# First block of a fused state-space and feed-forward kernel: running rows added by VectorE, branch stages respread

## The chip, the cores and the metric

The kernel runs on one core of a Trainium2 chip. The time is the device time of one execution in microseconds; the median of 3 runs of the kernel before is 490.83 us (490.7 to 491.28). Engines are named as in the profile: PE is TensorE (its weight loads are PEld), DVE is VectorE, ACT is ScalarE, POOL is GpSimd, SP is the queue that issues most DMAs.

## The reference

A sequence of L = 2048 tokens with D = 448 channels passes two branches, each behind a layer norm that is scaled and shifted by a modulation made from a vector `c`:

```python
mod = (_silu(c) @ w_mod).reshape(c.shape[0], 6, 1, -1)
sa, ca, ga, sb, cb, gb = (mod[:, 0], ..., mod[:, 5])
h = _layernorm(x, axis=-1) * (1 + ca) + sa
x = x + ga * _A_ref(h, ...)          # state-space convolution, N = 256 states, + h * Dskip
h = _layernorm(x, axis=-1) * (1 + cb) + sb
x = x + gb * _B_ref(h, w_gate, w_up, w_down)   # (silu(h @ w_gate) * (h @ w_up)) @ w_down, F = 1792
```

`_A_ref` forms `K[d, l] = Re sum_n C exp(l dt A) dt B` and convolves `h` with it causally, by FFT. Everything is float32.

## The kernel before, in words

**Tiles.** The 2048 tokens are 16 tiles of 128 rows (numbered 0 to 15) in six blocks of 2, 2, 3, 3, 3, 3 tiles. A block's tiles go through the feed-forward branch together (`ffn`), and while they do, the tiles of the *next* block go through the first branch in pieces put between. This case is about the first block: its feed-forward has tiles 0 and 1, and beside it run the first-branch stages of tiles 2 and 3, the "branch tiles".

**Feed-forward.** A loop over f = 0 to 13 (a "step") takes 128 of the 1792 hidden channels: `gate_up(f)` multiplies the transposed, normalised tokens by the gate and up weights on PE (L686; 22 matmuls into two PSUM banks of a ring of four, `bank`), ACT applies Silu (L701), DVE multiplies (L714), ACT casts the product to its high part (L717), DVE takes the low part (L718). Then `down(f-1)` (L730) adds the previous step's product with the down weights into the banks `dn`, in six matmuls per step with two tiles. High and low parts stand in for full float32 products. In the first block the weights are still being split: ACT casts gate and up weights (L120), DVE takes their remainders (L122, L124); the same for the down weights (L112, L114). So in the first block each step brings DVE five instructions of its own.

**First branch.** A flag computed on the chip selects the small path, which is the one that runs here: the kernel is taken as linear over the lag, so the convolution is two running sums over tokens. The stages of a branch tile i in the first block are: statistics of the first norm and their root on POOL (`n1.stat`, `n1.root`); `s0`, the normalised and modulated rows h (L184, L186); `s1`, the gated operands v0 = h * gm0 and v1 = h * gm1 (L859, on DVE); `s4f`, the sums over the tokens up to each row, as products with the triangle `tri` on PE, o in the bank `cv` from v0 (L897) and s in a ring bank from v1 (L896); `s5`, which carries the totals on and adds both sums to the tile. The totals of all earlier tokens are two "running rows" run0 and run1, row 0 of the tile `run`; they are added to every row as products of tri's first row with them (L898, L899: one row of operand, 448 columns). The carry copies the last rows of s (L908, ACT), adds o (L909, DVE) and moves row 127 of `run` to row 0 by a DMA that ACT's queue issues (L910). Then come the statistics of the second norm (`n2.stat`, L148 and L149), their root on POOL (`n2.root`, L165 to L172), the normalised tile on ACT (`make_xn`, L199), and after step 13's gate and up the transposes on PE (L206) with their evictions (L207 to L212), which the next block's first gate products need.

**What sets the order.** Each engine works its queue in the order in which the code is written; a wait at the head holds all that stands behind. The place of each stage is written out in numbers: `TIMES[b]` holds for block b the half-steps of the first statistics, of their root, of each stage of each branch tile (the last number is `n2.stat`), of the second root and of `make_xn`. A half-step h is step h // 2, behind `gate_up` and ahead of `down` where it is even, behind `down` where it is odd.

Of the kernel before, what the change touches and what calls it, by code (L numbers as in the profile page):

```python
# [12 lines left out]
OP = mybir.AluOpType  # L13
# [16 lines left out]


TIMES = (
# [3 lines left out]
)  # L36
# [16 lines left out]
def f32(ap):  # L53
    return ap.bitcast(F32)
# [3 lines left out]
def tile_kernel(ctx, tc, x, a_re, a_im, b_re, b_im, c_re, c_im, log_dt, dskip,  # L58
                wd, wgate_up, states, groups, vecs, dft, idft, out):
    nc = tc.nc  # L60
    sy, ve, sc, po, pe = nc.sync, nc.vector, nc.scalar, nc.gpsimd, nc.tensor
# [10 lines left out]
    def bank():  # L72
        t = psg.tile([128, 512], F32, name="bank")
        return t

    xs = {}
# [50 lines left out]
    tri = const.tile([128, 128], F32R)  # L127
    tok = const.tile([128, 1], F32)

    run = const.tile([128, 2, D], F32)  # L130
    run0, run1 = run[:, 0, :], run[:, 1, :]
# [49 lines left out]
    def make_h(h, i, part=None, ca=ca1, sh=sa):  # L181
        m, rs = n1.of[i][0:2]
        if part != 1:
            ve.scalar_tensor_tensor(h, xs[i], m, ca, op0=OP.subtract, op1=OP.mult)  # L184
        if part != 0:
            ve.scalar_tensor_tensor(h, h, rs, sh, op0=OP.mult, op1=OP.add)  # L186
# [57 lines left out]
    with tc.tile_pool(name="pre", bufs=1) as pre:  # L244
# [6 lines left out]
        for kind, q in ((n[0], n[1:]) for n in ORDER.split()):  # L251
# [3 lines left out]
            elif kind == "m":  # L255
                g, b = int(q[0]), (slice(0, 2 * D), slice(2 * D, NM))[int(q[1])]
# [52 lines left out]
        for q in range(2):  # L309
# [14 lines left out]
        h01, v0, v1, hd, h2 = ([pre.tile([128, w], t, name=f"{n}_{q}") for q in range(2)] for n, t, w in  # L324
                               (("h", F32, D), ("v0", F32, D), ("v1", F32R, D), ("hd", F32, D), ("h2", F32, 512)))
# [517 lines left out]
    def small_path(pools):  # L843
        work = pools.work
        vs = {}

        def s0(i):
            h = h_of(i)
            make_h(h, i)
            vs[i] = h  # L850

        def s1(i, on_v=False):
            h = vs[i]
            v0 = v0_of(i)
            v1 = work.tile([128, D], F32R, name="v1", bufs=2)
            for v, g in ((v0, gm0), (v1, gm1)):
                (ve if on_v else po).tensor_tensor(v, h, g, op=OP.mult)  # L859
            vs[i] = h, v0, v1  # L860

        def rows(i, on_v=False):
            h, v0, v1 = vs[i]
            ve.tensor_tensor(v0[0:1], v0[0:1], run0[0:1], op=OP.add)  # L864
            (ve if on_v else po).tensor_tensor(v1[0:1], f32(v1[0:1]), run1[0:1], op=OP.add)  # L865

        def s2(i, on_v=False):
            rows(i, on_v)
            h, v0, v1 = vs[i]
            vh = work.tile([128, D], F32R, name="vh")  # L870
            vl = work.tile([128, D], F32R, name="vl")
            sc.copy(vh, v0)  # L872
            ve.tensor_tensor(vl, v0, f32(vh), op=OP.subtract)
            vs[i] = h, vh, vl, v1

        def s3(i, on_v=False):
            h = vs[i][0]
            (ve if on_v else po).tensor_tensor(h, h, gd, op=OP.mult)

        def s4(i):  # L880
            h, vh, vl, v1 = vs[i]
            o = CV[:, 0:D]
            s = bank()[:, 0:D]
            pe.matmul(o, tri, vh, start=True, stop=False)  # L884
            pe.matmul(s, tri, v1, start=True, stop=True)  # L885
            pe.matmul(o, tri, vl, start=False, stop=True)  # L886
            ve.tensor_tensor(xs[i], h, xs[i], op=OP.add)
            vs[i] = o, s

        def s4f(i):
            h, v0, v1 = vs[i]
            o = CV[:, 0:D]
            s = bank()[:, 0:D]
            pe.matmul(s, tri, v1, start=True, stop=False)  # L896
            pe.matmul(o, f32(tri), v0, start=True, stop=False)  # L897
            pe.matmul(s, f32(tri[0:1, :]), run1[0:1], start=False, stop=True)  # L898
            pe.matmul(o, f32(tri[0:1, :]), run0[0:1], start=False, stop=True)  # L899
            s3(i, True)  # L900
            ve.tensor_tensor(xs[i], h, xs[i], op=OP.add)
            vs[i] = o, s

        def s5(i):
            o, s = vs.pop(i)
            if i + 1 < NT:
                e = slice(96, 128)
                sc.copy(run1[e], s[e])  # L908
                ve.scalar_tensor_tensor(run0[e], run1[e], 128.0, o[e], op0=OP.mult, op1=OP.add)  # L909
                sc.dma_start(run[0:1], run[127:128])  # L910
            ve.tensor_tensor(xs[i], xs[i], o, op=OP.add)
            ve.scalar_tensor_tensor(xs[i], s, tok, xs[i], op0=OP.mult, op1=OP.add)

        v = lambda g: lambda i: g(i, True)
        return lambda b: ((s0, v(s1), s4f, s5), (s0, v(s1), v(s2), v(s3), s4, s5),
                          (s0, s1, s2, s3, s4, s5))[min(b, 2)]

    def general_path(pools, y):
# [34 lines left out]
    with tc.If(rv > 0) as cond:  # L953
        with ExitStack() as es:
            pools = Pools(es)
            run_blocks(pools, small_path(pools))
# [65 lines left out]
```

## Time and profile before

| | us |
|---|---|
| median of 3 runs | 490.83 |
| the profiled execution | 490.99 |
| its span (first to last instruction on record) | 489.2 |
| PE busy | 481.9 (99% of the span) |
| DVE busy | 269.1 (55%) |
| ACT busy | 162.4 (33%) |
| POOL busy | 71.6 (15%) |
| the first block's loop on PE, from step 1 to the second block's first product | 41.74 to 98.88 |

The granted clock of PE is 0.997 over the span. In the rows of the timeline stand start, duration, engine, line, operation, output and inputs, shape and count; brackets hold the idle time of the engine before the row and what ended it.

### The profile page before, as it was taken

The page shows a single profiled execution, that of the slowest core. Times are in us where ns is not written, and L with a number is a line of the kernel's source. Part 1 is how long each engine was busy: PE and PEld are TensorE (multiplying, and loading weights), DVE is VectorE, ACT ScalarE, POOL GpSimd, SP SyncE. Part 2 cuts the span into 40 slices and gives each one's busy share as a digit, 9 for nine tenths or more (in the row PEclk, how much of TensorE's full clock was granted, in tenths as well). Part 3 has the DMA queues.
Part 4 walks back from the last instruction along what each step waited for, and adds up shares of the span by engine and source line. Part 5 has one row for each costly group of instructions (what it writes and reads, how often), then busy time and mean ns, then how long its engine had stood idle before and what let it go on. Part 6 is the DMA issues. An engine that isn't in the chain of part 4 may idle for free.

```text
span 489.2 us, 6961 instructions
## 1 busy us (share of the span) xinstructions
PE 481.9 (99%) x2765; PEld 452.4 (92%) x2765; DVE 269.1 (55%) x521; ACT 162.4 (33%) x350; POOL 71.6 (15%) x93
## 2 busy tenths in 40 slices
PE   8999999999999999999999999999999999999995
PEld 5649988999999999999999999999999999999995
DVE  4868999568885444634735553474555445222224
ACT  5665545622226112224411222531122161211111
POOL 2141001000000023411005150100623010000000
PEclk9999999999999999999999999999999999999998
DMA  8945662020000200000210000030000002000001
GB/s 311 405 166 151 226 198 87 21 95 1 0 3 3 93 1 0 2 1 2 73 41 1 2 0 2 0 114 1 0 2 1 1 0 76 21 1 0 1 0 62
DMA packets 12268, 26.50 MB, mean 54 GB/s; under 512 B 1858, under 2 KB 8131, under 8 KB 12227
## 3 DMA queue, kind: packets, MB, share of 16 engines
q1 hardware_dynamic: 11520, 25.79, 15.4%
q8 instruction: 23, 0.38, 0.3%
q10 hardware_dynamic: 706, 0.18, 0.2%
q14 instruction: 19, 0.15, 0.1%
HBM read 22.26 MB, written 3.67 MB: 53 GB/s over the span
## 4 chain that ended last, share of the span: by engine, by line
PE 95%; DMA 2%; DVE 1%; ACT 0%; SPq 0%; issue 0%; DVEq 0%
PE bank L686 59%; PE dn L730 27%; PE bank L225 2%; DMA wm<-in_w_mod_groups_dram 2%; PE bank L206 1%; PE dn L420 1%; DMA vec<-in_c_log_dt_dram 1%; PE bank L229 1%; PE cv L886 0%; PE cv L884 0%; PE bank L885 0%; PE cv L225 0%; PE bank L376 0%; PE bank L898 0%; DVE x L769 0%; PE cv L206 0%
## 5 line engine op out<-in xcount | busy, mean ns | idle before, releaser
L686 PE MATMUL bank<-hhi,gu 128*128 128x384 f32 (+1 forms) x1169 | 210.1, 318 | 0.0
L686 PEld LDWEIGHTS bank<-hhi,gu 128*128 128x128 f32 x1169 | 190.3, 188 | 3.2 <-issue 0.7
L686 PE MATMUL bank<-hlo,gu 128*128 128x384 f32 (+1 forms) x668 | 131.5, 318 | 0.0
L714 DVE TENSOR_TENSOR bank<-raw,bank 128x384 f32<-128x384 f32 (+1 forms) x69 | 36.9, 535 | 142.8 <-PE bank L686 127.6
L686 PEld LDWEIGHTS bank<-hlo,gu 128*128 128x128 f32 x668 | 109.6, 188 | 0.2 <-DVE hlo L212 0.2
L717 ACT CAST phi<-bank 128x384 fp32r<-128x384 f32 (+1 forms) x83 | 36.9, 445 | 144.7 <-DVE bank L714 144.7
L701 ACT ACTIVATE raw<-bank 128x384 f32<-128x384 f32 (+1 forms) x70 | 32.9, 469 | 121.1 <-PE bank L686 112.6
L718 DVE TENSOR_TENSOR plo<-bank,phi 128x384 fp32r<-128x384 f32 (+1 forms) x83 | 42.5, 512 | 37.5 <-ACT phi L717 37.5
L730 PE MATMUL dn<-wdh,phi 128*128 128x448 f32 x218 | 58.2, 368 | 0.0
L730 PE MATMUL dn<-wdh,plo 128*128 128x448 f32 x218 | 57.9, 366 | 0.0
L730 PE MATMUL dn<-wdl,phi 128*128 128x448 f32 x218 | 57.7, 366 | 0.0
L730 PEld LDWEIGHTS dn<-wdl,phi 128*128 128x128 f32 x218 | 40.9, 188 | 3.6
L730 PEld LDWEIGHTS dn<-wdh,plo 128*128 128x128 f32 x218 | 41.0, 188 | 3.5
L730 PEld LDWEIGHTS dn<-wdh,phi 128*128 128x128 f32 x218 | 38.4, 188 | 1.7 <-ACT run L908 0.7
L859 POOL TENSOR_TENSOR m<-m,gm 128x448 f32<-128x448 f32 x9 | 11.2, 1240 | 64.8 <-DVE m L186 55.3
L165 POOL TENSOR_SCALAR rsb<-mvb 128x3 f32<-128x3 f32 (+2 forms) x7 | 1.9, 275 | 120.5 <-DVE mvb L149 120.5
L165 POOL TENSOR_SCALAR rsa<-mva 128x3 f32<-128x3 f32 (+1 forms) x6 | 1.4, 231 | 105.5 <-DVE mva L149 105.5
L120 ACT CAST gu<-raw 128x1024 fp32r<-128x1024 f32 x14 | 14.6, 1045 | 0.0
L872 ACT CAST vh<-m 128x448 fp32r<-128x448 f32 x12 | 6.8, 568 | 22.3 <-DVE m L864 22.3
L865 POOL TENSOR_TENSOR v<-v,run 1x448 fp32r<-1x448 f32 x9 | 11.4, 1272 | 17.8 <-DMA run<-run 17.5
L225 PE MATMUL bank<-wm,cs 128*128 128x448 f32 x30 | 12.6, 550 | 0.2 <-DMA wm<-in_w_mod_groups_dram 0.2
L122 DVE TENSOR_TENSOR gu<-raw,gu 128x768 fp32r<-128x768 f32 x13 | 12.3, 950 | 0.0
(217 smaller groups left out, 433.5 us busy)
## 6 DMA issues: line engine op xcount, KB each, us to landing
raw<-in_B_w_gate_up_dram SPq DMA_DIRECT2D x14, 512.0 KB, 3.7
rawd<-in_B_w_down_dram SPq DMA_DIRECT2D x16, 224.0 KB, 3.8
x<-in_A_u_dram SPq DMA_DIRECT2D x12, 224.0 KB, 3.1
out_dram<-x SPq DMA_DIRECT2D x11, 224.0 KB, 1.9
wm<-in_w_mod_groups_dram SPq DMA_DIRECT2D x5, 448.0 KB, 8.1
wm<-in_w_mod_groups_dram SPq DMA_DIRECT2D x5, 336.0 KB, 7.9
rawd<-in_A_u_dram SPq DMA_DIRECT2D x4, 224.0 KB, 3.0
out_dram<-rawd SPq DMA_DIRECT2D x4, 224.0 KB, 1.9
```

What stands on the lines that cost most here:

```text
L120: sc.copy(wgu[j][:, :, 0:4, :], w)
L122: en.tensor_tensor(lo, w[:, :, 0:3, :], f32(hi), op=OP.subtract)
L225: pe.matmul(ps[:, 0:D], cs[:, k:k + 1].to_broadcast([128, 128]), w[:, k * D:(k + 1) * D], start=k == 0, stop=False)
L686: pe.matmul(ps[s][:, 0:n], w[:, s, a], (hlo if lo else hhi)[:, k, 0:n], start=first and q == 0, stop=end and q == len(ka) - 1)
L701: sc.activation(p[:, 0:n], ps[0][:, 0:n], AF.Silu)
L714: ve.tensor_tensor(ps[1][:, 0:n], p[:, 0:n], ps[1][:, 0:n], op=OP.mult)
L717: sc.copy(hi[:, 0:n], ps[1][:, 0:n])
L718: ve.tensor_tensor(lo[:, 0:n], ps[1][:, 0:n], f32(hi[:, 0:n]), op=OP.subtract)
L730: pe.matmul(dn[q][:, 0:D], u[:, cs], v, start=f == 0 and z == 0, stop=f == (NF - 3 if last else NF - 1) and z == 2)
L859: (ve if on_v else po).tensor_tensor(v, h, g, op=OP.mult)
L865: (ve if on_v else po).tensor_tensor(v1[0:1], f32(v1[0:1]), run1[0:1], op=OP.add)
L872: sc.copy(vh, v0)
```

## The change

The two one-row products of `s4f` (L898, L899) go. In their place the running rows are added on DVE to row 0 of v0 and v1 ahead of the products, by `rows`, which the later blocks already use (L864, L865). The last stage of a tile is cut in two: `s5f` holds the carry (`carry`, L903 to L905) and the addition of s times the token number (L910); `s6f` adds o (L914), multiplies h by `gd` (L878, until now in `s4f`) and adds it (L916). So the stages are six and not four, and `TIMES[0]` is a new table: the first root at half-step 2 and no longer 5; tile 2's stages at 4, 7, 9, 11, 11, 12 with its statistics at 13 (before: 5, 10, 15, 15 and 15); tile 3's at 8, 11, 16, 19, 19, 21 with its statistics at 22 (before: 9, 9, 18, 19 and 19); the second root at 22 (19); the normalised tiles at 24 and 25 (24 and 23).

```diff
 TIMES = (
-    ((1, 1), 5, ((5, 10, 15, 15, 15), (9, 9, 18, 19, 19)), 19, (24, 23)),
+    ((1, 1), 2, ((4, 7, 9, 11, 11, 12, 13), (8, 11, 16, 19, 19, 21, 22)), 22, (24, 25)),
...
         def s4f(i):
             h, v0, v1 = vs[i]
             o = CV[:, 0:D]
             s = bank()[:, 0:D]
-            pe.matmul(s, tri, v1, start=True, stop=False)
-            pe.matmul(o, f32(tri), v0, start=True, stop=False)
-            pe.matmul(s, f32(tri[0:1, :]), run1[0:1], start=False, stop=True)
-            pe.matmul(o, f32(tri[0:1, :]), run0[0:1], start=False, stop=True)
-            s3(i, True)
-            ve.tensor_tensor(xs[i], h, xs[i], op=OP.add)
-            vs[i] = o, s
-
-        def s5(i):
-            o, s = vs.pop(i)
+            pe.matmul(s, tri, v1, start=True, stop=True)
+            pe.matmul(o, f32(tri), v0, start=True, stop=True)
+            vs[i] = o, s, h
+
+        def carry(i, o, s):
             if i + 1 < NT:
                 e = slice(96, 128)
                 sc.copy(run1[e], s[e])
                 ve.scalar_tensor_tensor(run0[e], run1[e], 128.0, o[e], op0=OP.mult, op1=OP.add)
                 sc.dma_start(run[0:1], run[127:128])
+
+        def s5f(i):
+            o, s, h = vs[i]
+            carry(i, o, s)
+            ve.scalar_tensor_tensor(xs[i], s, tok, xs[i], op0=OP.mult, op1=OP.add)
+
+        def s6f(i):
+            o, s, h = vs.pop(i)
+            ve.tensor_tensor(xs[i], xs[i], o, op=OP.add)
+            s3(i, h, True)
+            ve.tensor_tensor(xs[i], h, xs[i], op=OP.add)
+
+        def s5(i):
+            o, s = vs.pop(i)
+            carry(i, o, s)
             ve.tensor_tensor(xs[i], xs[i], o, op=OP.add)
             ve.scalar_tensor_tensor(xs[i], s, tok, xs[i], op0=OP.mult, op1=OP.add)
...
-        return lambda b: ((s0, v(s1), s4f, s5), (s0, v(s1), v(s2), v(s3), s4, s5),
+        return lambda b: ((s0, v(s1), v(rows), s4f, s5f, s6f), (s0, v(s1), v(s2), v(s3), s4, s5),
                           (s0, s1, s2, s3, s4, s5))[min(b, 2)]
```

How the rows of the queues move is shown at three places. First PE at tile 2's sums; `v_...` and `m_78` are v1 and v0, `run` the running rows, `dn` and `gu` the down products and the gate and up weights. Before, behind `down` of step 7:

```order
L730 MATMUL dn_69<-wdh_659,plo 128x448
L896 MATMUL bank<-v_761,tri 128x448
L897 MATMUL cv<-m_78,tri 128x448
L898 MATMUL bank<-run,tri 128x448
L899 MATMUL cv<-run,tri 128x448
L686 MATMUL bank<-hhi,gu_657 128x256 x7
```

And in the changed kernel, behind `down` of step 5:

```order
L730 MATMUL dn_69<-wdh_559,plo 128x448
L896 MATMUL bank<-v_668,tri 128x448
L897 MATMUL cv<-m_78,tri 128x448
L686 MATMUL bank<-hhi,gu_557 128x256 x7
L686 MATMUL bank<-hlo,gu_557 128x256 x4
```

Two of the four products are gone, and the other two stand two steps earlier.

Second, DVE from step 4's end to step 5's end, where tile 3's `s0`, tile 2's row additions and the steps' own L114 to L124 meet (`x_74`, `x_75` are tiles 2 and 3; `wd` and `gu` the split weights). Before:

```order
L184 SCALAR_TENSOR_TENSOR m_78<-x_75,mva,ca_89 128x448
L186 SCALAR_TENSOR_TENSOR m_78<-m_78,rsa,sa 128x448
L859 TENSOR_TENSOR m_78<-m_78,gm_92 128x448
L859 TENSOR_TENSOR v_717<-m_78,g_91 128x448
L114 TENSOR_TENSOR wdl_607<-rawd_84,wdh_606 128x448
L714 TENSOR_TENSOR bank<-p,bank 128x256
L122 TENSOR_TENSOR gu_604<-raw_80,gu_604 128x2x384
L718 TENSOR_TENSOR plo<-bank,phi 128x256
L124 TENSOR_TENSOR gu_604<-raw_80,gu_604 64x2x128
L859 TENSOR_TENSOR m_78<-m_78,gm_92 128x448
L859 TENSOR_TENSOR v_761<-m_78,g_91 128x448
```

And now:

```order
L186 SCALAR_TENSOR_TENSOR m_78<-m_78,rsa,sa 128x448
L864 TENSOR_TENSOR m_78<-m_78,run 1x448
L865 TENSOR_TENSOR v_668<-v_668,run 1x448
L114 TENSOR_TENSOR wdl_611<-rawd_84,wdh_610 128x448
L714 TENSOR_TENSOR bank<-p,bank 128x256
L122 TENSOR_TENSOR gu_608<-raw_80,gu_608 128x2x384
L718 TENSOR_TENSOR plo<-bank,phi 128x256
L124 TENSOR_TENSOR gu_608<-raw_80,gu_608 64x2x128
L904 SCALAR_TENSOR_TENSOR run<-run,cv 32x448
L910 SCALAR_TENSOR_TENSOR x_74<-bank,tok,x_74 128x448
L859 TENSOR_TENSOR m_78<-m_78,gm_92 128x448
L859 TENSOR_TENSOR v_776<-m_78,g_91 128x448
```

The row additions stand where an `s1` stood, and carry and first addition of tile 2 have come into step 5, ahead of tile 3's `s1`.

Third, ACT in steps 11 to 13, where the normalised tiles (`raw_81`) are made between the steps' casts. Before:

```order
L717 CAST phi<-bank 128x256
L199 ACTIVATE raw_81<-x_75,ngb,rsb 128x448
L199 ACTIVATE raw_81<-x_75,ngb,rsb 128x64
L112 CAST wdh_963<-rawd_82 128x448
L701 ACTIVATE p<-bank 128x256
L717 CAST phi<-bank 128x256
L199 ACTIVATE raw_81<-x_74,ngb,rsb 128x448
L199 ACTIVATE raw_81<-x_74,ngb,rsb 128x64
L112 CAST wdh_1029<-rawd_83 128x448
```

And now:

```order
L112 CAST wdh_965<-rawd_82 128x448
L701 ACTIVATE p<-bank 128x256
L717 CAST phi<-bank 128x256
L199 ACTIVATE raw_81<-x_74,ngb,rsb 128x448
L199 ACTIVATE raw_81<-x_74,ngb,rsb 128x64
L199 ACTIVATE raw_81<-x_75,ngb,rsb 128x448
L199 ACTIVATE raw_81<-x_75,ngb,rsb 128x64
L112 CAST wdh_1017<-rawd_83 128x448
L701 ACTIVATE p<-bank 128x256
```

Both tiles are now made behind step 12's cast L717, ahead of step 13's L112 and Silu.

More of the change, by code (lines that the diff above doesn't have):

```diff
@@ L874, in s2, with s3 @@
             vs[i] = h, vh, vl, v1
-        def s3(i, on_v=False):
-            h = vs[i][0]
+        def s3(i, h=None, on_v=False):
+            h = vs[i][0] if h is None else h
             (ve if on_v else po).tensor_tensor(h, h, gd, op=OP.mult)
@@ L910, in s5 @@
                 sc.dma_start(run[0:1], run[127:128])
+        def s5f(i):
[10 more added lines that the diff above has]
+            carry(i, o, s)
             ve.tensor_tensor(xs[i], xs[i], o, op=OP.add)
             ve.scalar_tensor_tensor(xs[i], s, tok, xs[i], op0=OP.mult, op1=OP.add)
-        v = lambda g: lambda i: g(i, True)
-        return lambda b: ((s0, v(s1), s4f, s5), (s0, v(s1), v(s2), v(s3), s4, s5),
+        v = lambda g: lambda i: g(i, on_v=True)
+        return lambda b: ((s0, v(s1), v(rows), s4f, s5f, s6f), (s0, v(s1), v(s2), v(s3), s4, s5),
                           (s0, s1, s2, s3, s4, s5))[min(b, 2)]
```

## The prediction

> **What bounds the kernel now.** I read the page first, then the chain of waits, then the timeline of the first block engine by engine.
>
> ```profile
> PE 481.9 (99%) x2765; PEld 452.4 (92%) x2765; DVE 269.1 (55%) x521; ACT 162.4 (33%) x350; POOL 71.6 (15%) x93
> ...
> PE 95%; DMA 2%; DVE 1%; ACT 0%; SPq 0%; issue 0%; DVEq 0%
> ```
>
> TensorE is busy for 99% of the span and is 95% of the chain that ended last: whatever leaves its queue shortens the kernel, as long as nothing new makes it wait. VectorE's 55% is an average that hides the first block, so I asked for busy time by stretch.
>
> ```profile
> core 0: us, PE busy (x) PEld busy (x) DVE busy (x) ACT busy (x) POOL busy (x), PEclk, DMA share, GB/s
> 41.74:61.00 19.26, 19.26 (x145) 18.73 (x144) 16.86 (x33) 10.53 (x20) 1.53 (x2) 1.00 0.60 205
> 61.00:68.30 7.30, 7.30 (x56) 7.11 (x55) 7.18 (x15) 4.50 (x9) 0.00 (x0) 1.00 0.53 151
> ```
>
> In the columns (stretch, its length, then busy time of PE, PEld, DVE, ACT, POOL) the reader is to see that TensorE never pauses here, and that from 61.0 to 68.3 VectorE is busy for 7.18 of 7.30 us. It is as full as TensorE, in the very stretch into which the change puts more of it.
>
> **What TensorE sheds.** The first branch tile's matmuls:
>
> ```profile
> 68.34 0.37 PE L896 MATMUL bank<-v,tri 128*128 128x448 f32 x1
> 68.54 0.91 PE L897 MATMUL cv<-m,tri 128*128 128x448 f32 x2
> 69.39 1.01 PE L898 MATMUL bank<-run,tri 1*128 1x448 f32 x2
> 70.24 0.91 PE L899 MATMUL cv<-run,tri 1*128 1x448 f32 x2
> 71.08 1.09 PE L686 MATMUL bank<-hhi,gu 128*128 128x256 f32 x7
> ```
>
> The two one-row products L898 and L899 go. They hold TensorE from 69.39 to 71.08, 1.69 us, though their operand has one row. Two tiles: 2 x 1.69 = 3.38 us, all on the path, since TensorE waits for nothing around them. If that were all, the profiled execution (490.99 us, span 489.2) would come to 487.6.
>
> **What VectorE gains and when.** Durations on VectorE are start to start, since neighbours overlap:
>
> ```profile
> 54.51 0.63 DVE L114 TENSOR_TENSOR wdl<-rawd,wdh 128x448 fp32r<-128x448 f32 x1
> ...
> 58.08 0.68 DVE L184 SCALAR_TENSOR_TENSOR m<-x,mva,ca 128x448 f32<-128x448 f32 x1
> ...
> 59.52 0.63 DVE L859 TENSOR_TENSOR m<-m,gm 128x448 f32<-128x448 f32 x1
> 60.06 0.62 DVE L859 TENSOR_TENSOR v<-m,g 128x448 fp32r<-128x448 f32 x1
> 60.60 0.62 DVE L114 TENSOR_TENSOR wdl<-rawd,wdh 128x448 fp32r<-128x448 f32 x1
> 61.14 0.42 DVE L714 TENSOR_TENSOR bank<-p,bank 128x256 f32<-128x256 f32 x1
> ...
> 63.24 0.63 DVE L859 TENSOR_TENSOR m<-m,gm 128x448 f32<-128x448 f32 x1
> ```
>
> One step's own VectorE work (L114 to the next group) is 63.24 - 60.60 = 2.64 us, and L714 to that group 2.10; s0 is 59.52 - 58.08 = 1.44; s1 is 60.60 - 59.52 = 1.08, each of its two at 0.54, for 0.62 busy.
>
> ```profile
> 69.60 0.63 DVE L878 TENSOR_TENSOR m<-m,gd 128x448 f32<-128x448 f32 x1
> 70.26 0.62 DVE L901 TENSOR_TENSOR x<-m,x 128x448 f32<-128x448 f32 x1
> 71.27 0.63 DVE L909 SCALAR_TENSOR_TENSOR run<-run,cv 32x448 f32<-32x448 f32 x1 [0.38 <-PE cv L899]
> 71.92 0.62 DVE L911 TENSOR_TENSOR x<-x,cv 128x448 f32<-128x448 f32 x1
> 72.58 0.68 DVE L912 SCALAR_TENSOR_TENSOR x<-bank,tok,x 128x448 f32<-128x448 f32 x1
> 73.30 0.63 DVE L148 BATCH_NORM_STATS2 stb<-x 128x6 f32<-128x448 f32 x1
> ...
> 74.06 0.61 DVE L114 TENSOR_TENSOR wdl<-rawd,wdh 128x448 fp32r<-128x448 f32 x1
> ...
> 116.87 0.60 DVE L864 TENSOR_TENSOR m<-m,run 1x448 f32<-1x448 f32 x1
> 117.41 0.60 DVE L865 TENSOR_TENSOR v<-v,run 1x448 fp32r<-1x448 f32 x1
> ```
>
> An instruction that needs the one before starts 0.66 after it (L878 to L901); the statistics take 74.06 - 73.30 = 0.76. The added row additions are in the trace only in the next block: 0.60 us each for one row, 0.54 start to start. Four of them are new: 4 x 0.54 = 2.16 us. Bounds: 0 if they fell into idle time, 4 x 0.70 = 2.8 if none overlapped; I take 2.16, the rows being the same form.
>
> The rest of the change moves work, and VectorE's queue is in order, so I add up its whole queue. It is unchanged until 54.51, where s1 of tile 2 now stands before L114 of step 4. From there to L714 of step 11: seven steps and one L114, 7 x 2.64 + 0.54 = 19.02; s1 twice, 2.16; s0 of tile 3, 1.44; the row additions, 2.16; carry and the first part of the sum (L904, L910), twice 0.65 + 0.60 (0.68 less the overlap of 0.08) = 2.50; the second part (L914, L878, L916) with the statistics of tile 2, 0.54 + 0.66 + 0.66 + 0.76 = 2.62, and of tile 3, whose statistics come a step later, 1.74. Together 31.64 us.
>
> To that comes a wait for ScalarE, whose queue issues the carry's DMA only when L904 is done, ahead of the casts L112 and L120 of the same step:
>
> ```profile
> 81.24 0.63 DVE L909 SCALAR_TENSOR_TENSOR run<-run,cv 32x448 f32<-32x448 f32 x1
> ...
> 82.44 0.57 ACT L112 CAST wdh<-rawd 128x448 fp32r<-128x448 f32 x1 [2.27 <-DVE run L909]
> ...
> 83.38 1.04 ACT L120 CAST gu<-raw 128x1024 fp32r<-128x1024 f32 x1
> ...
> run<-run ACTq DMA_DIRECT2D x13, 3.5 KB, 1.7
> ```
>
> L112 ends 1.14 us after the carry's sum (83.01 against 81.87) and L120 2.55 after it. Before, four VectorE instructions stood behind the sum and covered this. For tile 2 the s1 of tile 3 still does; for tile 3 only L910 is left, so L114 waits some 0.5 and L122 another 0.5, 1.0 in all (bounds 0 and 1.1). The carry's DMA itself costs nothing: it lands a median 1.7 us after issue, and three steps lie between the carry of tile 2 and the reading of row 0 for tile 3.
>
> L714 of step 11 then starts at 54.51 + 31.64 + 1.0 = 87.2. TensorE, 3.38 ahead, would have let it start near 84.9 (88.23 before, in the next rows): VectorE is 2 us behind. Whether that costs anything is decided at the end of the block.
>
> **Where it comes due.** Tile 3's statistics now stand in step 11 (half-step 22 instead of 19), and both normalised tiles, which the transposes after step 13's gate and up need, are made on ScalarE in step 12:
>
> ```profile
> 83.94 0.18 DVE L149 BATCH_NORM_AGGREGATE mvb<-stb 128x2 f32<-128x6 f32 x1
> ...
> 85.98 0.25 POOL L172 TENSOR_SCALAR ngb<-ngb 128x2 f32<-128x2 f32 x1
> ...
> 88.23 0.43 DVE L714 TENSOR_TENSOR bank<-p,bank 128x256 f32<-128x256 f32 x1 [0.94 <-ACT gu L120]
> ...
> 88.96 1.09 ACT L199 ACTIVATE raw<-x,ngb,rsb 128x448 f32<-128x448 f32 x2
> 89.96 0.55 ACT L112 CAST wdh<-rawd 128x448 fp32r<-128x448 f32 x1
> ...
> 95.56 0.60 PE L206 MATMUL bank<-ident,raw 128*128 128x128 f32 x4
> 95.82 0.43 DVE L714 TENSOR_TENSOR bank<-p,bank 128x256 f32<-128x256 f32 x1 [0.86 <-PE bank L686]
> ...
> 99.46 0.41 DVE L212 TENSOR_TENSOR hlo<-bank,hhi 128x256 fp32r<-128x256 f32 x1
> ...
> 100.16 0.98 PE L686 MATMUL bank<-hhi,gu 128*128 128x256 f32 x7
> ```
>
> Statistics end at 87.2 + 2.10 + 0.84 = 90.1. GpSimd's root ends 2.11 after them (86.23 against 84.12): 92.2. ScalarE needs 1.00 a tile: 94.3. TensorE reaches the transposes at 95.56 - 3.38 = 92.2 and waits about 2 us, the gain's larger part. Behind the two tiles on ScalarE stand L112 and Silu of step 13; L112 ends near 94.85, L114 follows, and L714 of step 13 starts at 95.4, where it was 95.82. From that L714 hang the transposes' evictions, up to the last L212: 4.05 us to its end at 99.87, just ahead of the products before 100.16 that need it (some 0.1 us to spare). So what is left of 3.38 at the start of the second block is 0.4 + 0.1, about 0.5 us. From there nothing is changed: TensorE keeps this lead to the end.
>
> **The sum:** 3.38 shed, some 2.9 given back in waits. 490.99 - 0.5 = 490.5 for the profiled execution; the median of the runs is 0.16 lower, so 490.3.
>
> [...]
>
> **The rivals.**
> - *The lead is kept.* VectorE's lag stays hidden, as it did before with 7.18 of 7.30 us busy and no wait on TensorE. Full gain: 490.83 - 3.38 = 487.5. Against it: the statistics' new place binds even without lag (next).
> - *VectorE catches up by step 11,* because waits for ScalarE or the row additions fall into pauses. L714 of step 11 then starts at 84.9, statistics end at 87.8, the root at 89.9, the tiles at 91.95, L714 of step 13 at 93.05, where full gain needs 92.44: 0.6 lost, 0.1 of it spare, so 2.9 gained and 487.9. Anything between this and the forecast is possible; each 0.1 us of lag is 0.1 us of time. Against it: the queue's 31.64 is made of rows.
> - *VectorE's moved instructions do not overlap:* slower. Each then costs 0.66 instead of 0.54; s1, the row additions, L910 and the second part of both tiles are 14 instructions, 14 x 0.12 = 1.7 us more lag. The gain of 0.5 is gone at the fourth, and with all 14 it is 1.2 slower: 492.0. Against it stand the overlaps of L859 and L864.
> - *TensorE loses its clock in the 2 us wait:* slower.
>
> ```profile
> 1.58 5.26 PE L241 MATMUL bank<-tri 128*128 128x512 f32 x14 [1.58 <-DVE tri L274]
> ```
>
>  At the start, from rest, 128x512 matmuls take 5.26 / 14 = 0.376 us, where the steps' 128x256 take about 0.12 (7 in 0.98 with the last one's tail of 0.14), so 0.24 for twice the columns: 14 x 0.136 = 1.9 us lost in warming up. So 490.3 + 1.9 = 492.2. It needs a wait long enough; no wait like it is in the trace of before. [...]
>
> **How the numbers follow.** About 0.2% (1 us) is what a measurement of this kernel can tell from no change. Forecast 490.3: 0.53, within 0.2%, its own range 489.8 to 491.3. Lead kept 0.05 and catching up 0.21, both faster. No overlap 0.12 and clock 0.09, both slower. So faster 0.26, same 0.53, slower 0.21. Ends: the forecast's doubtful terms are the two waits for ScalarE (1.0 down to 0) and the row additions (2.16 down to 0), of which I let the gain take about 1.9: 488.4. Upward, half of the lost overlap and a little more: 491.7.
>
> **What would show it.** In the profile after: no L898/L899; four more row additions of about 0.6 us on VectorE, which is busy without a break from 54 to 80; L112 of step 10 idle-waiting for run L904; a wait of 1.5 to 2 us of TensorE's L206 ahead of the transposes, with the normalised tiles' L199 ending near 94; the row of 100.16 near 99.7. A wait at L896 for the row additions over 0.3 us, or L206 without a wait, would show the queue's sum wrong; a granted clock under 1.00 after the wait would show the fourth case.

## The result and the profile after

| | before | changed |
|---|---|---|
| median of 14 runs each, us | 491.12 | 490.6 |
| lowest, us | 490.7 | 490.09 |
| span of the profiled execution, us | 489.2 | 488.4 |

The ratio of changed to before is 0.9988, with a 95% interval from 0.9978 to 0.9999: by the medians 0.5 us faster, a gain that the interval only just tells from none. The profiled execution of the changed kernel is faster by 0.8 us of span.

The page of the changed kernel, engine totals and chain, and its list of TensorE's waits:

```profile
PE 480.2 (98%) x2757; PEld 451.8 (93%) x2757; DVE 270.6 (55%) x525; ACT 162.1 (33%) x350; POOL 71.4 (15%) x93
...
PE 90%; DVE 6%; issue 1%; ACT 1%; POOL 0%; ACTq 0%; DVEq 0%; POOLq 0%
```

```profile
PE bank L206 <- ACT raw L199: 1.0, 2, 0.7
...
PE bank L206 <- ACT p L701: 0.3, 1, 0.3
PE dn L730 <- ACT phi L717: 0.2, 1, 0.2
```

TensorE has shed eight matmul instructions (2765 to 2757), but the chain that ended last now runs through VectorE, ScalarE and GpSimd for a stretch, and waits stand at the transposes (L206) that were not there before.

The timeline of the changed kernel, VectorE's queue from the first moved instruction to the end of tile 3's statistics:

```profile
54.51 0.63 DVE L859 TENSOR_TENSOR m<-m,gm 128x448 f32<-128x448 f32 x1
...
59.55 0.61 DVE L864 TENSOR_TENSOR m<-m,run 1x448 f32<-1x448 f32 x1
60.09 0.61 DVE L865 TENSOR_TENSOR v<-v,run 1x448 fp32r<-1x448 f32 x1
60.62 0.61 DVE L114 TENSOR_TENSOR wdl<-rawd,wdh 128x448 fp32r<-128x448 f32 x1
...
81.67 0.62 DVE L114 TENSOR_TENSOR wdl<-rawd,wdh 128x448 fp32r<-128x448 f32 x1 [0.46 <-ACT wdh L112]
...
83.02 0.96 DVE L122 TENSOR_TENSOR gu<-raw,gu 128x768 fp32r<-128x768 f32 x1 [0.38 <-ACT gu L120]
...
87.07 0.42 DVE L714 TENSOR_TENSOR bank<-p,bank 128x256 f32<-128x256 f32 x1
...
89.83 0.18 DVE L149 BATCH_NORM_AGGREGATE mvb<-stb 128x2 f32<-128x6 f32 x1
```

The reader is to see that the row additions start 0.54 apart, that no wait stands on VectorE until 81.67 and then two for ScalarE, and that L714 of step 11 starts at 87.07. What follows from the statistics, in order of time, from the timelines of GpSimd, ScalarE, TensorE and VectorE of the same kernel:

```profile
91.79 0.25 POOL L172 TENSOR_SCALAR ngb<-ngb 128x2 f32<-128x2 f32 x1
...
91.93 0.63 PE L686 MATMUL bank<-hlo,gu 128*128 128x256 f32 x4
92.07 2.08 ACT L199 ACTIVATE raw<-x,ngb,rsb 128x448 f32<-128x448 f32 x4 [0.79 <-POOL ngb L172]
...
92.88 0.33 PE L206 MATMUL bank<-ident,raw 128*128 128x128 f32 x1 [0.33 <-ACT raw L199]
93.86 0.55 PE L206 MATMUL bank<-ident,raw 128*128 128x128 f32 x3 [0.65 <-ACT raw L199]
...
94.93 0.44 PE L206 MATMUL bank<-ident,raw 128*128 128x128 f32 x2 [0.30 <-ACT p L701]
...
95.18 0.42 DVE L714 TENSOR_TENSOR bank<-p,bank 128x256 f32<-128x256 f32 x1
...
97.64 1.09 PE L686 MATMUL bank<-hhi,gu 128*128 128x256 f32 x7
98.57 1.09 PE L686 MATMUL bank<-hlo,gu 128*128 128x256 f32 x4
98.80 0.42 DVE L212 TENSOR_TENSOR hlo<-bank,hhi 128x256 fp32r<-128x256 f32 x1
...
99.50 0.98 PE L686 MATMUL bank<-hhi,gu 128*128 128x256 f32 x7
```

The last row answers to the one at 100.16 before: TensorE enters the second half of the next block's first gate and up 0.66 us earlier, and that is all that is left of 3.38. Before, the two rows ahead of it, the first of the second block, were shorter:

```profile
98.88 0.98 PE L686 MATMUL bank<-hhi,gu 128*128 128x256 f32 x7
99.69 0.63 PE L686 MATMUL bank<-hlo,gu 128*128 128x256 f32 x4
```

Start to start, TensorE's loss can be followed. It is free for the transposes at 92.40 (91.93 + 0.47, the distance to the next row as from 99.69 to 100.16 before), 3.16 us earlier than before (95.56). From there to the second block's first product it takes 97.64 - 92.40 = 5.24 us, where it took 98.88 - 95.56 = 3.32: 1.92 lost. The first two rows of the second block take 99.50 - 97.64 = 1.86 us, where they took 100.16 - 98.88 = 1.28: 0.58 lost. In the second of them the weight load at 98.94 waits 0.17 us for an eviction (L212). 3.16 - 1.92 - 0.58 = 0.66. The brackets at L206 show only 1.28 of the 1.92, because they count idle time from a matmul's end and not from where the next one would have started.

For the experiments I use one measure beside the times: the stretch from step 1's first product to that row, "the block" below. It is free of what differs at a kernel's start. Before it is 100.16 - 41.74 = 58.42 us, after 99.50 - 41.73 = 57.77.

### The profile page after: what moved, and what is told of

Same layout as the page of the kernel before. It is cut to its first block, busy times and chain, and to the rows that moved or that the text cites. A ratio compares the mean times of both kernels' runs of the same rounds, so it can differ in the third digit from the quotient of the medians.

```text
span 488.4 us, 6949 instructions
## 1 busy us (share of the span) xinstructions
PE 480.2 (98%) x2757; PEld 451.8 (93%) x2757; DVE 270.6 (55%) x525; ACT 162.1 (33%) x350; POOL 71.4 (15%) x93
## 4 chain that ended last, share of the span: by engine, by line
PE 90%; DVE 6%; issue 1%; ACT 1%; POOL 0%; ACTq 0%; DVEq 0%; POOLq 0%
PE bank L686 54%; PE dn L730 25%; PE bank L225 2%; PE bank L241 1%; DVE gu L122 1%; PE dn L420 1%; PE bank L206 1%; PE bank L229 1%; DVE gu L124 1%; DVE bank L714 1%; DVE plo L718 1%; PE cv L886 1%; PE cv L884 1%; PE bank L885 0%; DVE wdl L114 0%
## 5 line engine op out<-in xcount | busy, mean ns | idle before, releaser
L714 DVE TENSOR_TENSOR bank<-raw,bank 128x384 f32<-128x384 f32 (+1 forms) x69 | 36.9, 535 | 143.1 <-PE bank L686 127.5
L717 ACT CAST phi<-bank 128x384 fp32r<-128x384 f32 (+1 forms) x83 | 36.9, 444 | 148.7 <-DVE bank L714 148.6
L701 ACT ACTIVATE raw<-bank 128x384 f32<-128x384 f32 (+1 forms) x70 | 32.9, 469 | 121.4 <-PE bank L686 117.1
L730 PE MATMUL dn<-wdh,phi 128*128 128x448 f32 x218 | 58.2, 368 | 0.2 <-ACT phi L717 0.2
L730 PE MATMUL dn<-wdh,plo 128*128 128x448 f32 x218 | 57.8, 366 | 0.0
L730 PE MATMUL dn<-wdl,phi 128*128 128x448 f32 x218 | 57.7, 366 | 0.0
L730 PEld LDWEIGHTS dn<-wdl,phi 128*128 128x128 f32 x218 | 40.9, 188 | 3.6
L730 PEld LDWEIGHTS dn<-wdh,plo 128*128 128x128 f32 x218 | 40.9, 188 | 3.5
L730 PEld LDWEIGHTS dn<-wdh,phi 128*128 128x128 f32 x218 | 38.4, 188 | 1.4 <-ACT phi L717 0.4
L859 POOL TENSOR_TENSOR m<-m,gm 128x448 f32<-128x448 f32 x9 | 11.2, 1240 | 64.8 <-DVE m L186 55.3
L865 POOL TENSOR_TENSOR v<-v,run 1x448 fp32r<-1x448 f32 x9 | 11.5, 1273 | 17.7 <-DMA run<-run 17.5
L122 DVE TENSOR_TENSOR gu<-raw,gu 128x768 fp32r<-128x768 f32 x13 | 12.2, 948 | 0.4 <-ACT gu L120 0.4
```

The costliest lines, as they stand in the source:

```text
L122: en.tensor_tensor(lo, w[:, :, 0:3, :], f32(hi), op=OP.subtract)
L701: sc.activation(p[:, 0:n], ps[0][:, 0:n], AF.Silu)
L714: ve.tensor_tensor(ps[1][:, 0:n], p[:, 0:n], ps[1][:, 0:n], op=OP.mult)
L717: sc.copy(hi[:, 0:n], ps[1][:, 0:n])
L730: pe.matmul(dn[q][:, 0:D], u[:, cs], v, start=f == 0 and z == 0, stop=f == (NF - 3 if last else NF - 1) and z == 2)
```

## The experiments

The theory behind all of them: what the change sheds on TensorE is 3.38 us; what it gets is decided by when tile 3's statistics end, because root, normalised tiles and evictions follow from there; and that is set by VectorE's queue and by the places written in the table.

| run | ratio to before, 95% interval | block from, to | block, us | against before |
|---|---|---|---|---|
| the kernel before | | 41.74, 100.16 | 58.42 | |
| the changed kernel | 0.9988 (0.9978 to 0.9999) | 41.73, 99.50 | 57.77 | -0.65 |
| e1 products out | 0.9935 (0.992 to 0.9949) | 41.78, 96.80 | 55.02 | -3.40 |
| e2 respread alone | 1.0024 (1.0014 to 1.0034) | 42.68, 102.25 | 59.57 | +1.15 |
| e3 rows on GpSimd | 1.0019 (1.0006 to 1.0031) | 41.95, 101.82 | 59.87 | +1.45 |
| e4 carry DMA on SyncE | 0.9963 (0.995 to 0.9975) | 42.59, 99.23 | 56.64 | -1.78 |
| e5 statistics earlier | 0.9975 (0.9965 to 0.9984) | 41.70, 98.70 | 57.00 | -1.42 |
| e6 places by queue sum | 0.9942 (0.9925 to 0.9959) | 42.49, 98.19 | 55.70 | -2.72 |
| e7 rows in old places | 1.0028 (1.0009 to 1.0047) | 42.02, 101.31 | 59.29 | +0.87 |
| e8 one long wait | 1.0091 (1.0069 to 1.0114) | 42.33, 105.09 | 62.76 | +4.34 |
| e9 no row additions | 0.9953 (0.994 to 0.9967) | 42.17, 98.17 | 56.00 | -2.42 |

**What TensorE sheds (e1).** The kernel before, less the one-row products:

```diff
-            pe.matmul(s, tri, v1, start=True, stop=False)
-            pe.matmul(o, f32(tri), v0, start=True, stop=False)
-            pe.matmul(s, f32(tri[0:1, :]), run1[0:1], start=False, stop=True)
-            pe.matmul(o, f32(tri[0:1, :]), run0[0:1], start=False, stop=True)
+            pe.matmul(s, tri, v1, start=True, stop=True)
+            pe.matmul(o, f32(tri), v0, start=True, stop=True)
```

> The kernel before with its four one-row products (L898, L899 of tiles 2 and 3) left out and nothing put in their place, so tiles 2 and 3 lack the running rows of the tiles ahead of them. Theory (the products hold TensorE for 1.69 us per tile and all of it is on the path, and the old places of the stages leave room for a TensorE that is 3.4 us ahead): 3.4 us faster than before, no wait of TensorE ahead of the transposes. Rival (the products are worth less, TensorE would wait elsewhere anyway): 0.5 us or less, with new waits on L730 or L206.

The block is 3.40 us shorter and the time 0.65% (3.2 us); no wait of TensorE stands in the block. The term of 3.38 holds, all of it on the path, and the old places carry a TensorE that is so far ahead. So the 2.7 us that the change does not keep are lost by what it adds and moves.

**The respread by itself (e2).** The changed kernel with the products back and without `rows`:

```diff
-            pe.matmul(s, tri, v1, start=True, stop=True)
-            pe.matmul(o, f32(tri), v0, start=True, stop=True)
+            pe.matmul(s, tri, v1, start=True, stop=False)
+            pe.matmul(o, f32(tri), v0, start=True, stop=False)
+            pe.matmul(s, f32(tri[0:1, :]), run1[0:1], start=False, stop=True)
+            pe.matmul(o, f32(tri[0:1, :]), run0[0:1], start=False, stop=True)
...
-        return lambda b: ((s0, v(s1), v(rows), s4f, s5f, s6f), (s0, v(s1), v(s2), v(s3), s4, s5),
+        return lambda b: ((s0, v(s1), lambda i: None, s4f, s5f, s6f), (s0, v(s1), v(s2), v(s3), s4, s5),
```

> The changed kernel with the one-row products back and without the row additions: only the stages are respread and the last one cut in two. Theory (the new places cost by themselves: tile 3's statistics in step 11, both normalised tiles in step 12): about 1.3 us slower than before, with TensorE waiting about 0.6 us for the normalised tiles and some 0.6 behind that. Rival (the respread is harmless and only the row additions cost): the time of before, no wait at L206.

0.24% slower, 1.15 us in the block: the new places, with the last stage cut in two, cost 1.2 us with nothing else changed. Three rows of e2's timelines show where:

```profile
84.43 0.62 DVE L114 TENSOR_TENSOR wdl<-rawd,wdh 128x448 fp32r<-128x448 f32 x1 [0.46 <-ACT wdh L112]
...
89.83 0.42 DVE L714 TENSOR_TENSOR bank<-p,bank 128x256 f32<-128x256 f32 x1
...
97.69 0.44 PE L206 MATMUL bank<-ident,raw 128*128 128x128 f32 x2 [0.30 <-ACT p L701]
```

L714 of step 11 starts 0.66 us later than before, once the block's start (42.68, 0.94 later) is taken off: 88.89 against 88.23. The two losses that I expected at 0.6 each are there, start to start: 0.57 from the first transpose to the second block's first product (96.52 to 100.41, where it was 95.56 to 98.88) and 0.56 in the first two rows behind that (100.41 to 102.25, where it was 98.88 to 100.16). But what the last transposes wait for is Silu (L701), which stands behind the normalised tiles in ScalarE's queue, and not the tiles themselves.

**The row additions by themselves (e9).** Left out of the changed kernel:

```diff
-        return lambda b: ((s0, v(s1), v(rows), s4f, s5f, s6f), (s0, v(s1), v(s2), v(s3), s4, s5),
+        return lambda b: ((s0, v(s1), lambda i: None, s4f, s5f, s6f), (s0, v(s1), v(s2), v(s3), s4, s5),
```

> The changed kernel with its four row additions left out and nothing in their place (tiles 2 and 3 lack the running rows of the tiles ahead of them): the price of the additions by themselves, without GpSimd. Theory (they are 2.16 us of VectorE's queue, of which TensorE's own time takes over after about 1.5): 2.1 us faster than before, tile 3's statistics ending about 1.5 us earlier than in the changed kernel, no wait at L730. Rival (the run on GpSimd failed because the additions' place in the queue costs nothing, and its loss has another source than GpSimd's work beside VectorE): the changed kernel's time, 0.5 us faster than before.

0.47% faster than before (2.3 us, where 2.1 were expected), the block 1.8 us shorter than the changed kernel's, and no wait at L730. The statistics of tile 3 end earlier too:

```profile
88.50 0.18 DVE L149 BATCH_NORM_AGGREGATE mvb<-stb 128x2 f32<-128x6 f32 x1
```

That is 1.8 us earlier (1.5 were expected) than 89.83 with the later start of this block (42.17 against 41.73) taken off. Four instructions of 0.54 us, on an engine that the page shows 55% busy, cost 1.8 us of the kernel's time.

**The wait for ScalarE (e4).** The first block's carry DMA from SyncE's queue:

```diff
-        def carry(i, o, s):
+        def carry(i, o, s, q=sc):
...
-                sc.dma_start(run[0:1], run[127:128])
+                q.dma_start(run[0:1], run[127:128])
...
-            carry(i, o, s)
+            carry(i, o, s, sy)
```

> The changed kernel with the first block's carry DMA issued from SyncE's queue and not from ScalarE's, so that L112 and L120 behind it no longer wait for L904. Theory (VectorE loses 0.84 us to that wait in step 10 and the chain to the end of the block is as much longer): 1.5 us faster than before, the idle time ahead of L114 and L122 of step 10 gone. Rival (the wait is hidden): the changed kernel's time, 0.5 us faster than before.

0.37% faster than before (1.8 us, where 1.5 were expected), 1.13 us in the block over the changed kernel. The same two rows of VectorE as at 81.67 and 83.02 in the changed kernel now have no wait:

```profile
81.91 0.62 DVE L114 TENSOR_TENSOR wdl<-rawd,wdh 128x448 fp32r<-128x448 f32 x1
...
82.77 0.95 DVE L122 TENSOR_TENSOR gu<-raw,gu 128x768 fp32r<-128x768 f32 x1
```

Start to start, L910 to L114 takes 0.60 us here and took 1.14 (80.53 to 81.67), and L714 to L122 takes 0.33 and took 0.80 (82.22 to 83.02): 1.01 us together, a little more than the 0.84 of the brackets. What ScalarE did in the changed kernel:

```profile
80.53 0.50 ACTq L905 DMA_DIRECT2D run<-run  x1
81.07 0.57 ACT L112 CAST wdh<-rawd 128x448 fp32r<-128x448 f32 x1 [1.93 <-DVE run L904]
```

A DMA of 3.5 KB cost a microsecond, not by its transfer but by standing in ScalarE's queue, with its wait for VectorE (to 80.53) and then 0.50 us for its issue, ahead of two casts for which VectorE waits. How the microsecond divides between the wait and the issue, e4 does not show, since it takes both away.

**The deadline (e5).** Tile 3's second part and statistics one step earlier:

```diff
-    ((1, 1), 2, ((4, 7, 9, 11, 11, 12, 13), (8, 11, 16, 19, 19, 21, 22)), 22, (24, 25)),
+    ((1, 1), 2, ((4, 7, 9, 11, 11, 12, 13), (8, 11, 16, 19, 19, 20, 20)), 20, (24, 25)),
```

> The changed kernel with tile 3's second part and statistics at half-step 20 and not 21 and 22, the second root at 20 too; nothing else. Theory (the statistics' time, through root, normalised tiles and evictions, sets the start of the second block; they move forward by as much as the one L114 to L124 group now behind them, TensorE pays a little at L730 of step 11): 1.45 us faster than before, 0.9 faster than the changed kernel. Rival (VectorE's whole queue sets the end whatever the order in it): the changed kernel's time, 0.5 us faster than before.

0.25% faster than before (1.2 us); the block comes out at -1.42 where -1.45 was expected. VectorE's amount of work is the same as in the changed kernel. The place of tile 3's second part and statistics in its queue is worth 0.8 us of the block by itself.

**One part alone (e7).** The kernel before with the row additions in place of the products, and nothing respread:

```diff
-    ((1, 1), 5, ((5, 10, 15, 15, 15), (9, 9, 18, 19, 19)), 19, (24, 23)),
+    ((1, 1), 5, ((5, 10, 13, 15, 15, 15), (9, 9, 17, 18, 19, 19)), 19, (24, 23)),
...
-        return lambda b: ((s0, v(s1), s4f, s5), (s0, v(s1), v(s2), v(s3), s4, s5),
+        return lambda b: ((s0, v(s1), v(rows), s4f, s5), (s0, v(s1), v(s2), v(s3), s4, s5),
```

(with the four lines of e1 for the products)

> The kernel before with the one-row products replaced by the row additions on VectorE (at half-steps 13 and 17) and every other stage where it was: the one part of the change without the respread. Theory (tile 3's products at half-step 18 then wait for its row additions, VectorE being 3 us behind by step 8): 0.65 us faster than before with one wait of about 2.7 us at L896; if such a wait costs TensorE its clock, as one of 2.0 us did in the run with the row additions on GpSimd, some 1.6 us more, so 1 us slower. Rival (the respread is needed for nothing): 2.7 us faster or more.

0.28% slower, where 1 us (0.2%) was forecast if the clock goes. The wait stands where the queue sum put it, and the clock falls at its end. From the waits and from the windows of e7 (stretch, length, busy times by engine, then the granted clock):

```profile
PE bank L896 <- DVE v L865: 2.8, 1, 2.8
```

```profile
76.00:78.00 2.00, 0.12 (x2) 0.00 (x0) 1.96 (x5) 1.96 (x4) 0.00 (x0) 1.00 0.00 0
78.00:80.00 2.00, 1.04 (x2) 0.83 (x3) 2.00 (x5) 0.37 (x2) 0.00 (x0) 0.69 0.62 141
80.00:82.00 2.00, 2.00 (x5) 1.29 (x4) 1.93 (x4) 0.62 (x2) 0.00 (x0) 0.50 0.94 328
82.00:84.00 2.00, 2.00 (x15) 1.90 (x15) 1.87 (x3) 0.11 (x1) 0.00 (x0) 0.96 0.06 22
```

The wait alone would have left a gain, and the clock takes it back. Of the eleven runs of e7, one had a mean granted clock of 0.999 and took 490.36 us, 0.9 faster than the median of before beside it (491.24), where 0.65 was forecast without a loss of the clock; the other ten had 0.990 to 0.996 and took 491.34 to 495.51. So the respread does what the row additions need: without it TensorE waits 2.8 us in one piece, and with the clock that this cost in most runs the kernel is slower.

**The row additions on GpSimd (e3), a miss.**

```diff
+        def rows_p(i):
+            h, v0, v1 = vs[i]
+            po.tensor_tensor(v0[0:1], v0[0:1], run0[0:1], op=OP.add)
+            po.tensor_tensor(v1[0:1], f32(v1[0:1]), run1[0:1], op=OP.add)
...
-        return lambda b: ((s0, v(s1), v(rows), s4f, s5f, s6f), (s0, v(s1), v(s2), v(s3), s4, s5),
+        return lambda b: ((s0, v(s1), rows_p, s4f, s5f, s6f), (s0, v(s1), v(s2), v(s3), s4, s5),
```

> The changed kernel with its four row additions on GpSimd, which is idle there, and no longer on VectorE. Theory (VectorE's queue is the chain up to tile 3's statistics, so 2.16 us less of it moves the statistics by 1.5, until TensorE's own time binds): 2.1 us faster than before, TensorE's wait ahead of the transposes down from 1.3 in all to about 0.8. Rival (the place of the statistics alone makes the wait, whatever VectorE does): the changed kernel's time, 0.5 us faster than before.

Neither: 0.19% slower than before, while e9 shows that the additions off VectorE's queue give what the theory said, and a little more. The timelines of GpSimd, VectorE and TensorE of e3:

```profile
55.49 1.42 POOL L869 TENSOR_TENSOR m<-m,run 1x448 f32<-1x448 f32 x1 [8.03 <-ACT p L701]
55.81 1.58 DVE L114 TENSOR_TENSOR wdl<-rawd,wdh 128x448 fp32r<-128x448 f32 x1
56.88 1.52 POOL L870 TENSOR_TENSOR v<-v,run 1x448 fp32r<-1x448 f32 x1
...
57.32 0.42 DVE L714 TENSOR_TENSOR bank<-p,bank 128x256 f32<-128x256 f32 x1
57.65 1.57 DVE L122 TENSOR_TENSOR gu<-raw,gu 128x768 fp32r<-128x768 f32 x1
...
69.63 0.92 DVE L883 TENSOR_TENSOR m<-m,gd 128x448 f32<-128x448 f32 x1
70.58 1.46 DVE L921 TENSOR_TENSOR x<-m,x 128x448 f32<-128x448 f32 x1
...
74.24 0.68 PE L730 MATMUL dn<-wdh,phi 128*128 128x448 f32 x2 [2.03 <-ACT phi L717]
```

Beside GpSimd's additions four VectorE instructions are longer: L114 1.58 for 0.62, L122 1.57 for 0.95, L883 (the product with gd) 0.92 and L921 (its addition) 1.46, each for 0.62. That is 0.96 + 0.62 + 0.30 + 0.84 = 2.72 us more, where 2.16 were to be saved. Not every overlap costs: the L859 at 55.28, which began before GpSimd's first addition and ran beside it for 0.4 us, kept its 0.62. Tile 3's additions fall ahead of step 7's L714, so the L730 that adds step 7's product waits 2.03 us (0.17 in the changed kernel), and behind that wait the granted clock is at 0.50, as e3's windows show:

```profile
74.00:75.50 1.50, 1.26 (x5) 1.12 (x6) 1.44 (x4) 1.50 (x4) 0.00 (x0) 0.89 0.00 0
75.50:77.00 1.50, 1.50 (x8) 1.43 (x7) 1.50 (x3) 0.91 (x3) 0.00 (x0) 0.50 0.43 60
77.00:78.00 1.00, 1.00 (x6) 1.00 (x6) 0.97 (x3) 0.31 (x1) 0.00 (x0) 0.50 0.69 266
78.00:79.00 1.00, 1.00 (x9) 1.00 (x8) 0.71 (x2) 0.46 (x2) 0.00 (x0) 0.72 0.90 354
```

That is the profiled run. The twelve runs of e3 part into two groups: seven took 492.49 to 493.51 us, six of them at a mean granted clock of 0.994, the profiled one among these; five took 490.84 to 491.90 us at 0.997 to 1.0, about the time of before beside them (median 491.26). So, as far as times and mean clocks tell, GpSimd's additions cost the gain, and the clock, where it falls, makes the kernel slower than before.

**The clock (e8).** One long wait:

```diff
-    ((1, 1), 2, ((4, 7, 9, 11, 11, 12, 13), (8, 11, 16, 19, 19, 21, 22)), 22, (24, 25)),
+    ((1, 1), 2, ((4, 7, 9, 11, 11, 12, 13), (8, 11, 16, 19, 19, 21, 26)), 26, (26, 26)),
```

> The changed kernel with tile 3's statistics, the second root and both normalised tiles put behind step 13's gate and up (half-step 26), so that TensorE waits once, ahead of the transposes, for about 6.7 us. Theory by the queues alone: 3.65 us slower than before. With a clock that falls to half for some 3.3 us after a wait of 2 us or more: 1.6 us on top, 5.3 slower, and the granted clock near 0.5 in the stretch after the wait.

0.91% slower, 4.34 us in the block, between the two forecasts. The wait was shorter than I had added up, 4.7 and 0.5 us, since GpSimd's root took 1.63 us from 95.37 and the first transpose needs tile 2 only. The clock did fall:

```profile
95.00:97.00 2.00, 0.00 (x0) 0.00 (x0) 0.25 (x2) 0.00 (x0) 1.38 (x4) 0.67 0.00 0
97.00:99.00 2.00, 0.64 (x2) 0.35 (x3) 0.00 (x0) 1.96 (x4) 0.01 (x1) 0.50 0.00 0
99.00:101.00 2.00, 2.00 (x9) 1.96 (x10) 1.01 (x3) 1.76 (x5) 0.00 (x0) 0.50 0.00 0
101.00:103.00 2.00, 2.00 (x8) 1.78 (x8) 1.60 (x4) 1.17 (x3) 0.00 (x0) 0.62 0.00 0
```

From the means, half clock lasts 1.32 + 2 + 2 + 1.52 = 6.84 us here, and some 4.2 us of TensorE's work fall into it, 2.1 us lost. As an estimate, 3.65 less the 1.5 us by which the wait was shorter, plus 2.1, is 4.25, near the measured 4.34. But the two errors of my sum stand against each other, so e8 shows the fall and its length, not its price.

**Other places (e6).** The row additions stay on VectorE; only the table differs from the changed kernel, with places picked by adding up the queues as the prediction does:

```diff
-    ((1, 1), 2, ((4, 7, 9, 11, 11, 12, 13), (8, 11, 16, 19, 19, 21, 22)), 22, (24, 25)),
+    ((1, 1), 2, ((4, 6, 7, 11, 11, 12, 15), (9, 11, 12, 19, 19, 19, 19)), 19, (23, 24)),
```

> The changed kernel, row additions on VectorE as they are, with places chosen by adding up the queues: tile 2 at 4, 6, 7, 11, 11, 12 and statistics at 15, tile 3 at 9, 11, 12, 19, 19, 19 and 19, second root at 19, normalised tiles at 23 and 24. Theory (a deadline, not VectorE's amount of work, costs the gain; every L714 to L718 still comes before its L730 but for two waits of 0.4 and 0.2): 2.7 us faster than before, no wait at L206. Rival (VectorE has too much work in the block for TensorE to keep its lead): 1 us or less.

0.58% faster than before, the block 2.72 us shorter where 2.7 was expected. Tile 3's statistics and one normalised tile, and TensorE's only wait in the block (two, of 0.4 and 0.2, were expected):

```profile
84.40 0.18 DVE L149 BATCH_NORM_AGGREGATE mvb<-stb 128x2 f32<-128x6 f32 x1
...
88.39 1.09 ACT L199 ACTIVATE raw<-x,ngb,rsb 128x448 f32<-128x448 f32 x2
...
73.25 0.67 PE L730 MATMUL dn<-wdh,phi 128*128 128x448 f32 x2 [0.50 <-ACT phi L717]
```

By the ratios it beats the kernel before by 2.8 us and the changed one by some 2.3 (by the block 2.7 and 2.1), with the same instructions on every engine as the changed one.

## Why the prediction was right, point by point

- **The sum.** 0.5 us faster was predicted, against before, and 0.5 was measured. The terms: shed 3.38, shown by e1 (3.40 in the block); given back 2.9 predicted, 2.7 measured.
- **VectorE's queue.** L714 of step 11 at 87.2 predicted, 87.07 measured. Its waits for ScalarE were put at 1.0; they are 0.46 + 0.38 = 0.84 in brackets and 1.01 start to start, and e4 shows them to be on the path, worth 1.1 us in the block. The row additions, 2.16 in the sum, are worth 1.8 us (e9).
- **Where it comes due.** Statistics end 90.1 predicted, 90.01 measured; root 92.2 and 92.04; tiles 94.3 and 94.15; L714 of step 13 95.4 and 95.18; the row of 100.16 near 99.7, measured 99.50. e5 confirms that the statistics' place is the lever. The "0.1 us to spare" ahead of that row was not there: L714 of step 13 came 0.64 earlier, the last L212 and the row 0.66.
- **TensorE's wait at L206.** "About 2 us" is right as the time lost from the transposes to the second block's first product, 1.92, but not as a wait: 0.33, 0.65 and 0.30 are idle, in three pieces. I let all transposes wait for both tiles; the first of them needs tile 2 alone, and the last waited for Silu, behind the tiles. The sum did not change by it, because behind the transposes the first products lost another 0.58 at their evictions, and these set the row of 99.50.
- **Catching up by step 11.** The floor under the new places, 0.5 us lost without lag, could not be seen alone: e2 lost 1.15, of which 0.66 is lag of L714, which leaves 0.5, an estimate by subtraction.
- **No overlap.** The moved instructions start 0.54 apart (59.55, 60.09, 60.62). The case is out.
- **The clock.** It stayed at 1.00 (92 to 100 us of the changed kernel), but 0.09 for losing it was too little for the wait that I forecast: the profiled runs of e3 and e7 lost the clock with waits of 2.03 and 2.8 us, and so, by their times and mean clocks, did most others of the two. Had the wait come in one piece of 2 us, as I had it, the clock may well have gone, and the time have been longer by an estimated 1.7 us, half of the 3.4 that the granted clock stayed at 0.50 in e3 and e7. I had put this at 1.9, from the kernel's first products (L241); they take 0.376 us each on average, but at a granted clock of 1.00 in the trace of before (1.58 to 6.84), so they show no fall of it. That the wait came in three pieces, which I had not foreseen, probably spared it; no run tests that alone. On this point the forecast was lucky.

## What to carry to other kernels

An engine's share of busy time says little about what an added instruction costs; its queue, added up from the row where it changes to the deadline that follows from it, gave each of these changes to some 0.3 us while neither GpSimd's work nor the clock interfered. An unbroken wait on TensorE of 2.03 us (e3) and of 2.8 us (e7) cost the profiled runs an estimated 1.7 us beyond its length, half of the 3.4 us at a granted clock of 0.50, and that in some runs and not in others. When work is respread, look for what the last statistics or the last input of the *next* stage waits behind, and put that early. A small DMA with a wait should not stand in the queue of an engine whose next results are waited for (e4: 1.13 us of the block for one of 3.5 KB).

## What the hardware did that I had not expected

- TensorE's granted clock fell to 0.50 with an unbroken wait of 2.03 us (e3) and of 2.8 us (e7), and stayed there for 3.4 us in both (from the windows' means: 0.33 + 1.5 + 1.0 + 0.56 in e3, 1.24 + 2.0 + 0.16 in e7); with waits of 4.7 and 0.5 us (e8) it stayed for 6.84, twice as long. Reckoned back from these means, as one step from 1.00 to 0.50, it fell 2.6 to 3.0 us after TensorE went idle (e3: idle from 72.21, fall at 75.17; e7: 76.11 and 78.76; e8: 93.13 and 95.68), in e3 0.9 us after the wait was over. The same wait does not always do it: by the times and mean clocks, five of e3's twelve runs and one of e7's eleven were spared. Waits of 0.33, 0.65 and 0.30 us within 2.5 us left it at 1.00 (the changed kernel). What decides between these cases the runs do not show.
- Beside a GpSimd addition on one partition, four VectorE instructions with two SBUF operands lasted longer (e3: L114 1.58 us for 0.62, L122 1.57 for 0.95, L883 0.92 and L921 1.46 for 0.62). The one at 57.32, which has one operand in PSUM, kept its 0.42; but the L859 at 55.28, with two in SBUF, kept its 0.62 as well. What decides between them the runs do not show.
